# Rows without a number column, values ahead of the back transposes, and three routing steps a place, in a chunk-attention, top-1 MoE and SiLU-MLP kernel

## The chip, the cores and the metric

The kernel runs on one core of one Trainium2 chip, as one program. Its engines are TensorE (PE; PEld is its weight load), VectorE (DVE), ScalarE (ACT), GpSimd (POOL) and SyncE (SP, which issues most DMAs). They run side by side, each through its own list of instructions in order, and wait for one another on semaphores. The metric is the time of one execution in microseconds on the device; lower is better.

## The reference: what is computed

Three layers follow one another, in float32. Chunked attention with 8 memory keys, a window of 16 to the left and 8 to the right:

```python
B, H, S, D = 4, 8, 768, 64
for c in range(S // 32):
    q_c = q[:, :, c * 32:c * 32 + 32]
    k_full = concat([mem_k, k[:, :, max(0, c * 32 - 16):min(S, c * 32 + 40)]])
    v_full = concat([mem_v, v[:, :, ...]])
    a = softmax(q_c @ k_full^T / sqrt(D))
    out[:, :, c * 32:c * 32 + 32] = a @ v_full
x = out.transpose(0, 2, 1, 3).reshape(3072, 512)
```

Then a mixture of 8 experts, of which each token takes the best one, with a gate from normalised logits:

```python
logits = unit(x) @ unit(expert_emb).T / tau
expert_idx = argmax(logits, axis=1)
gate_w = softmax(logits)[arange(N), expert_idx]
for e in range(8):
    out[mask_e] = gate_w[mask_e] * (relu(x[mask_e] @ w1[e]) @ w2[e])   # 512 -> 1024 -> 512
```

Then a dense MLP, `h = x @ w_in` (512 to 2048), `h * sigmoid(h)`, `@ w_out` (2048 to 512).

## The kernel before, in words

The order of the work on every engine is written out by hand, by the order in which the Python code records instructions.

**Attention** (`scores`, `exps`, `turned`, `values`, `columns`, `logits`, `logits2`) runs in 32 units `u`. A unit is one pair of heads (4 pairs a batch, 4 batches) and one half of the sequence, 384 tokens. In the loop over `u` several units are in flight: `scores(u)` multiplies q with the windows of k (PE, L780), DVE takes the maximum and subtracts it (L789, L792), ACT takes the exponential (`exps`, L797), `turned(u-1)` transposes the last unit's weights (PE, L803) and copies them (ACT, L805), `values(u-2)` multiplies by v (PE, L815) and DVE divides into `xb` (L827 to L831), and `columns(u-3)` transposes the result (PE, L849) and copies it to `xs` (ACT, L850). DVE and ACT also lay out the windows of k for the next pair (`kbuf`, L708). After the last pair of heads of a half, `logits(u-3)` multiplies `xs` by the expert vectors (PE, L864), DVE copies that (`ls`, L873), and `logits2(u-4)`, in the next unit, transposes it back (PE, L881) for a sum on DVE (L883). So two units of each batch hold a `logits` and the two after them a `logits2`. The half's rows are written from `xb` to the DRAM buffer `xd` by SP (L839).

`xd` has 3072 rows of 513 numbers, 2052 bytes: 512 values and the token's number, which POOL copies into `xb` (L825). `ys`, the DRAM buffer of the experts' results, has rows of the same form.

**Routing** is a list of small generators (`ranks`, `leading`, `places`, `gates`, `compact`) in `pending`. `advance(n)` runs the next `n` steps (up to each `yield`) at a place in the other work. `RATE`, here 2, is the number of steps at a place from the fifth unit before the last on. A step that yields `HOLD` keeps the next one back until a later place where PE may be used. `leading` picks two experts' first 256 tokens each (`pre`, two slots of two tiles of 128 rows): it ends in `pre_i`, a list of token numbers (L346), from which POOL gathers rows of `xd` (`gather`, L148). `places` then puts every other token at a place in slots of three or two tiles and leaves `ixs`, the token number at each of NA = 34 x 128 places. `compact` makes `rows_i`, the places in use, by way of the tile `wideh` (L558 to L564).

**The experts** run slot by slot (`step`, `firsts`, `seconds`), eight slices of the hidden layer each. Weights arrive in float32 and are split in a high and a low part by ACT and DVE (L92, L93); each product is three matmuls (`three`, L97 to L99). `turn` transposes the gathered rows (L170) and splits them. `first_mm` copies the number column aside (`ids`, L176), `second_mm` copies it behind the results (L196), and `put` writes the tile to `ys` (L201).

**The MLP** takes tokens in groups of four tiles. `pick` gathers a tile from `ys` (L1048), `pick_gate` takes the number column as integers (`tok_i`, L1056) and gathers the gates from `gd` by it (L1057), `gated` scales, `turn2` transposes, and `give` scatters the result by `tok_i` to the output (L1182).

Of the kernel before, what the change touches and what calls it, by code (L numbers as in the profile page):

```python
# [39 lines left out]
NF2 = FF2 // P  # L40
XW = DM + 1

# [16 lines left out]
def tile_chunk_attention_top1_moe_silu_mlp(ctx, tc, qT, kT, vW, emb, tau, wm, wo, out, dbg=None):  # L59
# [7 lines left out]
    psum = ctx.enter_context(tc.tile_pool(name="psum", bufs=1, space=PSUM))  # L67
    xd = dram.tile([N, XW], F32, name="xd")
    NY = N3 * 3 * P + N2 * 2 * P
    ys = dram.tile([NY + 3 * P, XW], F32, name="ys")  # L70
    gd = dram.tile([N, 1], F32, name="gd")
    bank = [psum.tile([P, DM], F32, name=f"bank{i}") for i in range(8)]

# [14 lines left out]
    meta_i = const.tile([1, LAST2 + 1], I32, name="meta_i")  # L88
    ids = const.tile([P, 3, 1], F32, name="ids")

# [26 lines left out]
    def space(pool, tag, nt):  # L117
        xs = tuple(pool.tile([P, KD, nt * P], F32R, name=f"x{n}{tag}") for n in "hl")
        hs = [tuple(pool.tile([P, nt * P], F32R, name=f"h{n}{tag}{i}") for n in "hl") for i in range(2)]
        return dict(x=xs, h=hs, row=pool.tile([P, nt, XW], F32, name=f"xrow{tag}"))  # L120

# [51 lines left out]
    def first_mm(s, f):  # L173
        n = s.nt * P
        if f == 0:
            DVE.tensor_copy(ids[:, 0:s.nt], s.where["row"][:, 0:s.nt, DM:])  # L176
        wh, wl = w1s[f % 2]
        xh, xl = s.where["x"]
        h = bank[2 + f % 2][:, 0:n]
        for k in range(KD):  # L180
            c = slice(k * P, (k + 1) * P)
            three(h, (wh[:, c], wl[:, c]), (xh[:, k, 0:n], xl[:, k, 0:n]), k == 0, k == KD - 1)
        hh, hl = (t[:, 0:n] for t in s.where["h"][f % 2])
        ACT.activation(hh, h, AF.Relu)  # L184
        DVE.scalar_tensor_tensor(hl, h, 0.0, hh.bitcast(F32), op0=ALU.max, op1=ALU.subtract)  # L185

    def second_mm(s, f):
        hh, hl = s.where["h"][f % 2]
        for c in range(s.nt):
            t = slice(c * P, (c + 1) * P)  # L190
            three(bank[s.acc + c], (hh[:, t], hl[:, t]), w2_of(s, f), f == 0, f == NF - 1)
        if f == NF - 1:
            y = s.y()
            for c in range(s.nt):
                if c == 1:
                    DVE.tensor_copy(y[:, 0:s.nt, DM:], ids[:, 0:s.nt])  # L196
                (DVE.tensor_copy if c % 2 else ACT.copy)(y[:, c, 0:DM], bank[s.acc + c])

# [285 lines left out]
    def places(home):  # L484
# [55 lines left out]
        for k in range(1, N3 + 1):  # L540
            out_ = rows2_i if k == N3 else ixp
            DVE.scalar_tensor_tensor(out_, ixs[:, 3 * k:3 * k + NA], here[:, k:k + 1], ixp, op0=ALU.mult, op1=ALU.add)
            yield

    def compact():

# [119 lines left out]

    SPOTS, HOLD, RATE, LASTW, GP = (2, 6), 2, 2, 1, 2

# [6 lines left out]
    with ExitStack() as a:  # L675
# [132 lines left out]
        def values(u):  # L808
# [14 lines left out]
            if half == 0 and pr == 0:  # L823
                xb[b] = xp.tile([P, TPB, XW], F32, tag="xb", name=f"xb{b}")
                POOL.tensor_copy(xb[b][:, :, DM:], token[:, b * TPB:(b + 1) * TPB])  # L825
            den = sm.tile([P, G, 2, 1], F32, tag="den", name=f"den{u}")
# [64 lines left out]
        for u in range(NU + 2):  # L891
# [8 lines left out]
            if u == 4:  # L900
                expert_columns()
            if 0 <= u - 4 < NU - 2 and place(u - 4)[3] == NPAIR - 1:
                logits2(u - 4)
            if ahead < NJ:
# [5 lines left out]
            if 0 <= u - 1 < NU:  # L910
                turned(u - 1)
            if 0 <= u - 3 < NU:
                columns(u - 3)
            if 0 < u < NU:
                exps(u)
            if 0 <= u - 2 < NU and u != NU:
                values(u - 2)
            advance(1 if u < NU - 5 else RATE, pe=True)
            if 0 <= u - 3 < NU and place(u - 3)[3] == NPAIR - 1:
# [26 lines left out]
        for i in range(1, NF - 2):  # L946
            ahead_of(pre[0], i)
            firsts(pre[0], i)
            if i == 1:
                logits2(NU - 1)  # L950
                pending.extend([places(bank[6]), gates(), compact()])
            seconds(pre[0], i)
            for b, t in squares[:2]:
                square(b, t)
            del squares[:2]
    lg = ex.enter_context(tc.tile_pool(name="lg", bufs=1, side="right"))
    large = [space(lg, "l", 3)]
    large.append(dict(large[0], x=tuple(lg.tile([P, KD, 3 * P], F32R, name=f"x{n}m") for n in "hl")))
    yfirst = [lg.tile([P, 2, XW], F32, name=f"yfirst{n}") for n in range(2)]
    w2d = tuple(lg.tile([P, DM], F32R, name=f"v2{n}3") for n in "hl")  # L960
# [22 lines left out]
    ypool = ctx.enter_context(tc.tile_pool(name="ypool", bufs=1))  # L983
    ymore = ypool.tile([P, 4, XW], F32, name="ymore")
    POOL.memset(ymore, 0.0)
# [14 lines left out]
    yr = [y[:, c] for y in yfirst for c in range(2)]  # L1000
    tok_i = [yrow.tile([P, TG], I32, name=f"tok{g}") for g in range(NG)]
    gt = [yrow.tile([P, TG], F32, name=f"gt{i}") for i in range(2)]
# [43 lines left out]
    def pick(g, c):  # L1046
        t = (g - 1) * TG + c
        POOL.indirect_dma_start(  # L1048
            out=yr[c],
            out_offset=None,  # L1050
            in_=ys[0:NA * P],
            in_offset=IndirectOffsetOnAxis(ap=rows_i[:, t:t + 1], axis=0),
        )

    def pick_gate(g, c):
        DVE.tensor_copy(tok_i[g][:, c:c + 1], yr[c][:, DM:])  # L1056
        POOL.indirect_dma_start(  # L1057
# [239 lines left out]
```

## Time and profile before

| | us |
|---|---|
| median of 3 runs | 1032.03 (1029.16 to 1032.31) |
| profiled execution | 1033.47, its span 1031.8 |
| PE busy | 977.9 (95%) |
| DVE busy | 617.2 (60%) |
| ACT busy | 463.9 (45%) |
| POOL busy | 147.4 (14%) |
| granted TensorE clock, mean | 0.988 |

Busy times are of the profiled execution. A row of a timeline gives start, duration, engine, line, operation, output<-input, and in brackets for how long the engine stood idle before it and which work ended that wait. PEclk is the clock that TensorE was granted, as a share of full speed, and a DMA share is the mean busy share of the 16 DMA engines.

### The profile page before, as it was taken

To read this page: it belongs to the slowest core of one execution; us is meant where nothing else is said; L and a number is where in the kernel's file an instruction comes from. 1 tells how busy PE (TensorE), PEld (TensorE's weight loads), DVE (VectorE), ACT (ScalarE), POOL (GpSimd) and SP (SyncE) were. 2 spreads that over 40 slices of the span, in tenths; PEclk is the share of its full clock that TensorE was granted. 3 is DMA by queue.
4 is the path that set the end of the run, shared out by engine and by line. 5 is a ranking of instruction groups with operands and counts; after the bars stand their busy time and mean duration, and the time that the engine had idled before them with its cause. 6 is when DMAs were issued, how large, how long until landed. Compare 5 with 4: busy or idle time off the path is not lost. (4 is left out here: it accounts for less than half of the span.)

```text
span 1031.8 us, 16881 instructions
## 1 busy us (share of the span) xinstructions
PE 977.9 (95%) x6365; PEld 824.8 (80%) x6365; DVE 617.2 (60%) x1274; ACT 463.9 (45%) x890; POOL 147.4 (14%) x209
## 2 busy tenths in 40 slices
PE   6788798999999999998999999999999999999995
PEld 4566677899988989997878888888888888888884
DVE  8788788777777888895999952332332232223230
ACT  8667566454456565664453433222322332232230
POOL 6133122110002000100310002021021002101001
PEclk9999999999999999999999999999999999999998
DMA  8989756664678887877443301020011002001001
GB/s 303 285 262 287 255 164 223 206 215 159 199 240 253 261 261 244 276 228 227 149 123 102 102 1 41 1 82 1 1 49 34 1 11 72 1 1 42 1 1 41
DMA packets 43537, 139.40 MB, mean 135 GB/s; under 512 B 5780, under 2 KB 5804, under 8 KB 43444
## 3 DMA queue, kind: packets, MB, share of 16 engines
q1 hardware_dynamic: 36596, 118.24, 35.7%
q0 software_dynamic: 6848, 19.97, 6.4%
q8 instruction: 53, 0.87, 0.3%
q14 instruction: 40, 0.33, 0.1%
HBM read 115.33 MB, written 22.85 MB: 134 GB/s over the span
## 5 line engine op out<-in xcount | busy, mean ns | idle before, releaser
L1159 DVE TENSOR_TENSOR sg<-bank,sg 128x512 f32<-128x512 f32 x96 | 66.2, 690 | 222.0 <-ACT sg L1154 222.0
L1154 ACT ACTIVATE sg<-bank 128x512 f32<-128x512 f32 x96 | 57.3, 597 | 258.9 <-PE bank L99 258.9
L93 DVE TENSOR_TENSOR gl<-sg,gh 128x512 fp32r<-128x512 f32 x92 | 63.8, 693 | 51.7 <-ACT gh L92 50.2
L97 PE MATMUL bank<-yh,w2bh 128*128 128x512 f32 x240 | 94.5, 394 | 0.0
L99 PE MATMUL bank<-yh,w2bl 128*128 128x512 f32 x240 | 93.5, 390 | 0.0
L98 PE MATMUL bank<-yl,w2bh 128*128 128x512 f32 x240 | 93.4, 389 | 0.0
L92 ACT CAST gh<-sg 128x512 fp32r<-128x512 f32 x92 | 57.1, 621 | 67.1 <-DVE sg L1159 67.1
L97 PE MATMUL bank<-w2bh,gh 128*128 128x512 f32 x224 | 87.3, 390 | 0.0
L99 PE MATMUL bank<-w2bh,gl 128*128 128x512 f32 x224 | 87.2, 389 | 0.0
L98 PE MATMUL bank<-w2bl,gh 128*128 128x512 f32 x224 | 87.1, 389 | 0.0
L97 PE MATMUL bank<-v2h,hhl 128*128 128x512 f32 x200 | 81.0, 405 | 0.0
L93 DVE TENSOR_TENSOR w1l<-raw,w1h 128x512 fp32r<-128x512 f32 x106 | 73.0, 689 | 12.6 <-ACT w1h L92 9.5
L184 ACT ACTIVATE hhl<-bank 128x256 fp32r<-128x256 f32 (+1 forms) x88 | 36.3, 412 | 95.6 <-PE bank L99 91.6
L99 PE MATMUL bank<-v2h,hll 128*128 128x512 f32 x200 | 79.0, 395 | 0.0
L98 PE MATMUL bank<-v2l,hhl 128*128 128x512 f32 x200 | 78.8, 394 | 0.0
L93 DVE TENSOR_TENSOR v2l<-raw,v2h 128x512 fp32r<-128x512 f32 x106 | 72.9, 688 | 0.0
L97 PE MATMUL bank<-xhl,w1h 128*128 128x256 f32 (+1 forms) x224 | 68.5, 306 | 1.4 <-DVEq L1124 1.4
L98 PE MATMUL bank<-xll,w1h 128*128 128x256 f32 (+1 forms) x224 | 68.4, 306 | 1.4 <-DVE xll L93 1.4
L185 DVE SCALAR_TENSOR_TENSOR hll<-bank,hhl 128x256 fp32r<-128x256 f32 (+1 forms) x88 | 40.3, 458 | 49.0 <-ACT hhl L184 48.5
L99 PE MATMUL bank<-xhl,w1l 128*128 128x256 f32 (+1 forms) x224 | 68.3, 305 | 0.0
L92 ACT CAST v2h<-raw 128x512 fp32r<-128x512 f32 x106 | 65.8, 621 | 1.2 <-PE bank L99 1.2
L92 ACT CAST w1h<-raw 128x512 fp32r<-128x512 f32 x106 | 65.1, 614 | 2.3 <-DMA raw<-in_wm_dram 2.3
(309 smaller groups left out, 2334.1 us busy)
## 6 DMA issues: line engine op xcount, KB each, us to landing
raw<-in_wm_dram SPq DMA_DIRECT2D x109, 512.0 KB, 4.6
coded<-in_wo_dram SPq DMA_DIRECT2D x36, 512.0 KB, 4.4
vbuf<-in_vW_dram SPq DMA_DIRECT2D x32, 390.0 KB, 6.2
k<-in_kT_dram SPq DMA_DIRECT2D x16, 400.0 KB, 7.5
xd<-xb SPq DMA_DIRECT2D x8, 769.5 KB, 7.7
q<-in_qT_dram SPq DMA_DIRECT2D x16, 384.0 KB, 6.0
ys<-ymore SPq DMA_DIRECT2D x8, 513.0 KB, 8.0
ys<-yfirst SPq DMA_DIRECT2D x7, 513.0 KB
```

The source lines that it names most:

```text
L92: ACT.copy(hi, src)
L93: eng.tensor_tensor(lo, src, hi.bitcast(F32), op=ALU.subtract)
L97: PE.matmul(out, lhsT=lh, rhs=rh, start=start, stop=False)
L98: PE.matmul(out, lhsT=lh, rhs=rl, start=False, stop=False)
L99: PE.matmul(out, lhsT=ll, rhs=rh, start=False, stop=stop)
L184: ACT.activation(hh, h, AF.Relu)
L185: DVE.scalar_tensor_tensor(hl, h, 0.0, hh.bitcast(F32), op0=ALU.max, op1=ALU.subtract)
L1154: ACT.activation(sg, h, AF.Sigmoid)
L1159: DVE.tensor_tensor(sg, h, sg, op=ALU.mult)
```

## The change: three things

1. The number column goes: rows of `xd`, `ys` and the tiles have 512 numbers (2048 bytes), and the copies into and out of the column go with it. Instead `names`, a new generator between `gates` and `compact`, transposes `ixs` and writes it to a DRAM buffer `td`, with `wideh` as its staging tile; `pick` gathers the numbers from `td` with a second indirect DMA. The first group's numbers are `pre_i` itself.
2. In the loop over units, `columns(u-3)` moves from before `exps(u)` and `values(u-2)` to behind them, and `logits2(u-4)` from before the windows of k to behind `turned(u-1)`.
3. `RATE` is 3 instead of 2.

```diff
-    xd = dram.tile([N, XW], F32, name="xd")
+    xd = dram.tile([N, DM], F32, name="xd")
...
-    ys = dram.tile([NY + 3 * P, XW], F32, name="ys")
+    ys = dram.tile([NY + 3 * P, DM], F32, name="ys")
...
+    td = dram.tile([NA * P, 1], I32, name="td")
...
     def first_mm(s, f):
         n = s.nt * P
-        if f == 0:
-            DVE.tensor_copy(ids[:, 0:s.nt], s.where["row"][:, 0:s.nt, DM:])
...
             for c in range(s.nt):
-                if c == 1:
-                    DVE.tensor_copy(y[:, 0:s.nt, DM:], ids[:, 0:s.nt])
-                (DVE.tensor_copy if c % 2 else ACT.copy)(y[:, c, 0:DM], bank[s.acc + c])
+                (DVE.tensor_copy if c % 2 else ACT.copy)(y[:, c], bank[s.acc + c])
...
+    def names():
+
+        yield HOLD
+        by_tile = bank[7][0:NA, 0:P]
+        PE.transpose(by_tile, ixs[:, 0:NA], ident)
+        yield
+        names_t = wideh.rearrange("p t e -> p (t e)")[0:NA, 0:P].bitcast(I32)
+        DVE.tensor_copy(names_t, by_tile)
+        SP.dma_start(out=td.rearrange("(t p) o -> t (p o)", p=P), in_=names_t)
+        yield
...
-    SPOTS, HOLD, RATE, LASTW, GP = (2, 6), 2, 2, 1, 2
+    SPOTS, HOLD, RATE, LASTW, GP = (2, 6), 2, 3, 1, 2
...
-                xb[b] = xp.tile([P, TPB, XW], F32, tag="xb", name=f"xb{b}")
-                POOL.tensor_copy(xb[b][:, :, DM:], token[:, b * TPB:(b + 1) * TPB])
+                xb[b] = xp.tile([P, TPB, DM], F32, tag="xb", name=f"xb{b}")
...
-            if 0 <= u - 4 < NU - 2 and place(u - 4)[3] == NPAIR - 1:
-                logits2(u - 4)
             if ahead < NJ:
                 windows(ahead, 1, u % 2)
                 windows(ahead, 0, u % 2)
...
                 turned(u - 1)
-            if 0 <= u - 3 < NU:
-                columns(u - 3)
+            if 0 <= u - 4 < NU - 2 and place(u - 4)[3] == NPAIR - 1:
+                logits2(u - 4)
             if 0 < u < NU:
                 exps(u)
             if 0 <= u - 2 < NU and u != NU:
                 values(u - 2)
+            if 0 <= u - 3 < NU:
+                columns(u - 3)
             advance(1 if u < NU - 5 else RATE, pe=True)
...
-                pending.extend([places(bank[6]), gates(), compact()])
+                pending.extend([places(bank[6]), gates(), names(), compact()])
...
-    tok_i = [yrow.tile([P, TG], I32, name=f"tok{g}") for g in range(NG)]
+    tok_i = [yrow.tile([P, TG], I32, name=f"tok{g}") if g else pre_i for g in range(NG)]
...
+        POOL.indirect_dma_start(
+            out=tok_i[g][:, c:c + 1],
+            out_offset=None,
+            in_=td,
+            in_offset=IndirectOffsetOnAxis(ap=rows_i[:, t:t + 1], axis=0),
+        )
 
     def pick_gate(g, c):
-        DVE.tensor_copy(tok_i[g][:, c:c + 1], yr[c][:, DM:])
```

How the order moves at three places. First PE at the logits of the first batch, before (bank_75 is the logits' bank, e the scores' exponentials, xb the attention's result, et the transposed weights):

```order
L864 MATMUL bank_75<-xs_0_391,enT 32x384 x4
L780 MATMUL bank_68<-kbuf_204,q_521 32x128 x12
L881 MATMUL bank_75<-ident,ls_0_719 128x128 x3
L803 MATMUL bank_71<-ident,e_682 128x128 x3
L849 MATMUL bank_74<-ident,xb_360 128x128 x3
L815 MATMUL bank_72<-vbuf_206,et_691 32x130 x12
L864 MATMUL bank_75<-xs_1_449,enT 32x384 x4
```

and of the change, where bank_76 is that bank:

```order
L869 MATMUL bank_76<-xs_0_407,enT 32x384 x4
L786 MATMUL bank_69<-kbuf_204,q_520 32x128 x12
L809 MATMUL bank_72<-ident,e_681 128x128 x3
L886 MATMUL bank_76<-ident,ls_0_718 128x128 x3
L821 MATMUL bank_73<-vbuf_206,et_690 32x130 x12
L854 MATMUL bank_75<-ident,xb_360 128x128 x3
L869 MATMUL bank_76<-xs_1_465,enT 32x384 x4
```

The back transposes of the logits (ls) stand behind the score transposes (e), and the transposes of the result (xb), whose copy the logits read, stand between the values and the logits.

Second DVE in the last units of attention, where `leading` ends, before (ev to ah are steps of routing, den and xb the division, mx the next maximum):

```order
L334 TENSOR_SCALAR bh<-count,ab 128x128 x2
L827 TENSOR_SCALAR den_1856<-bank_73 128x6
L354 SCALAR_TENSOR_TENSOR ev<-count_of,down 128x8
L356 TENSOR_REDUCE e_141<-ev 128x1
L829 RECIPROCAL den_1856<-den_1856 128x6
L358 TENSOR_SCALAR two<-r_mv,e_141 128x18
L359 TENSOR_SCALAR chosen_i<-e_141 1x1
L361 SCALAR_TENSOR_TENSOR st<-two,ab 128x18
L831 TENSOR_TENSOR xb_1675<-bank_73,den_1856 128x3x128
L365 TENSOR_SCALAR ah_153<-st,row 128x18
...
L344 TENSOR_SCALAR ix_154<-bank_75 128x2
L789 TENSOR_REDUCE mx_1946<-bank_69 128x6
L346 TENSOR_TENSOR pre_i<-ix_154,bank_75 128x2
```

and of the change:

```order
L329 TENSOR_SCALAR bh<-count,ab 128x128 x2
L349 SCALAR_TENSOR_TENSOR ev<-count_of,down 128x8
L714 COPY kbuf_204<-k_1619 64x12x56
L351 TENSOR_REDUCE e_141<-ev 128x1
L353 TENSOR_SCALAR two<-r_mv,e_141 128x18
L354 TENSOR_SCALAR chosen_i<-e_141 1x1
L356 SCALAR_TENSOR_TENSOR st<-two,ab 128x18
L832 TENSOR_SCALAR den_1853<-bank_74 128x6
L360 TENSOR_SCALAR ah_153<-st,row 128x18
...
L339 TENSOR_SCALAR ix_154<-bank_76 128x2
L341 TENSOR_TENSOR pre_i<-ix_154,bank_76 128x2
L795 TENSOR_REDUCE mx_1958<-bank_70 128x6
```

The routing steps stand ahead of the division of that unit, and pre_i ahead of the last maximum.

Third DVE between the gates and the places in use, before (seg is the staging tile of the gates):

```order
L586 RECIPROCAL gate<-gate 128x24
L592 COPY seg<-bank_75 24x128
L547 TENSOR_TENSOR lens<-rem,wide 128x8
L549 TENSOR_TENSOR lens<-rem,lens 128x8
L405 SCALAR_TENSOR_TENSOR cends<-lens,countf 128x16
L407 TENSOR_TENSOR cfirst<-cends,lens 128x16
L553 TENSOR_TENSOR skip<-row_167,cfirst 128x8
L554 TENSOR_TENSOR skip<-row_168,cfirst 128x8
L558 TENSOR_TENSOR wideh<-token,cfirst 128x320
```

and of the change:

```order
L592 RECIPROCAL gate<-gate 128x24
L598 COPY seg<-bank_76 24x128
L547 CAST wideh<-bank_76 34x128
L553 TENSOR_TENSOR lens<-rem,wide 128x8
L555 TENSOR_TENSOR lens<-rem,lens 128x8
L400 SCALAR_TENSOR_TENSOR cends<-lens,countf 128x16
L402 TENSOR_TENSOR cfirst<-cends,lens 128x16
L559 TENSOR_TENSOR skip<-row_167,cfirst 128x8
L560 TENSOR_TENSOR skip<-row_168,cfirst 128x8
L564 TENSOR_TENSOR wideh<-token,cfirst 128x320
```

The copy of the numbers into wideh is new, and seven instructions later wideh is written again.

## Rows read from the trace of the kernel before

**Rows 1.** The page's busy times, shares of the span and instructions.

```profile
PE 977.9 (95%) x6365; PEld 824.8 (80%) x6365; DVE 617.2 (60%) x1274; ACT 463.9 (45%) x890; POOL 147.4 (14%) x209
```

**Rows 2.** Stretches: start:end and length, busy by engine (instructions), PEclk, DMA share, GB/s.

```profile
26.00:32.00 6.00, 5.60 (x140) 4.39 (x136) 5.50 (x14) 4.83 (x10) 1.16 (x4) 1.00 0.86 294
40.00:50.00 10.00, 5.10 (x111) 4.06 (x111) 5.71 (x19) 3.73 (x10) 1.31 (x4) 0.91 1.03 281
50.00:60.00 10.00, 9.86 (x168) 7.78 (x168) 7.75 (x22) 8.38 (x20) 1.76 (x6) 0.75 0.75 283
70.00:80.00 10.00, 7.36 (x142) 5.79 (x145) 7.84 (x23) 5.93 (x16) 1.31 (x4) 0.94 1.00 300
80.00:90.00 10.00, 9.59 (x199) 7.54 (x192) 8.36 (x25) 8.18 (x19) 2.36 (x7) 0.88 0.89 316
118.00:130.00 12.00, 8.92 (x54) 7.04 (x45) 6.62 (x15) 5.05 (x11) 0.00 (x0) 0.86 0.88 251
190.00:1031.80 841.80, 822.87 (x4129) 701.29 (x4127) 459.95 (x822) 338.88 (x626) 90.19 (x91) 0.99 0.34 109
```

**Rows 3.** Timeline of 33 to 49 us: the write to xd and a late k.

```profile
33.21 3.05 SPq L839 DMA_DIRECT2D xd<-xb  x2
...
48.17 0.51 DVE L708 COPY kbuf<-k 64x672 f32<-64x672 f32 x1 [3.25 <-DMA k<-in_kT_dram]
```

**Rows 4.** DMA: slices of 38:46, 486:494, 1021:1027 us; issues, KB each, us to landing.

```profile
DMA  9959999999979979397696999999159959799989
GB/s 123 133 123 226 154 174 164 123 113 103 82 103 133 108 92 103 51 135 99 58 161 151 183 178 193 117 225 115 63 195 348 353 174 316 251 292 442 364 348 427
...
GB/s 41 41 0 0 0 226 380 431 349 369 390 236 226 205 143 123 307 369 307 348 205 61 123 164 410 471 369 348 410 348 348 123 82 0 0 0 0 0 0 82
...
GB/s 0 0 0 0 0 0 0 0 0 0 0 0 0 0 55 355 410 410 410 109 0 0 0 0 0 0 0 0 0 0 0 0 0 0 0 0 0 0 0 0
...
raw<-in_wm_dram SPq DMA_DIRECT2D x109, 512.0 KB, 4.6
...
xd<-xb SPq DMA_DIRECT2D x8, 769.5 KB, 7.7
...
out_dram<-o,tok POOLq DMA_INDIRECT x24, 2.7
ymore<-ys,rows_i POOLq DMA_INDIRECT x20, 3.7
```

**Rows 5.** Timeline of 95 to 99 us: a unit that ends in logits.

```profile
95.72 0.89 PE L864 MATMUL bank<-xs,enT 128*32 128x384 f32 x8
...
97.39 0.55 DVE L789 TENSOR_REDUCE mx<-bank 128x6 f32<-128x384 f32 x1
97.52 0.31 PEld L881 LDWEIGHTS bank<-ident,ls 128*128 128x128 f32 x3 [0.53 <-DVE ls L873]
...
98.24 0.49 PE L849 MATMUL bank<-ident,xb 128*128 128x128 f32 x3
...
98.81 0.49 ACT L850 COPY xs<-bank 128x384 f32<-128x384 f32 x1
```

**Rows 6.** Timeline of 113 to 123 us: the first slot's gather.

```profile
113.41 0.14 DVE L346 TENSOR_TENSOR pre_i<-ix,bank 128x2 int32<-128x2 f32 x1
...
115.34 0.95 POOL L148 DMA_INDIRECT xrows<-xd,pre_i  x1 [0.30 <-issue]
...
122.92 1.48 PE L170 MATMUL bank<-ident,xrows 128*128 128x128 f32 x7 [2.49 <-DMA xrows<-xd,pre_i]
```

**Rows 7.** Timeline of 178 to 186 us: gates, places in use, first slot of three tiles.

```profile
178.84 0.66 PE L170 MATMUL bank<-ident,xrowl 128*128 128x128 f32 x4 [0.95 <-DMA xrowl<-xd,rows_i]
...
181.32 0.28 DVE L592 COPY seg<-bank 24x128 f32<-24x128 f32 x1 [0.37 <-PE bank L589]
...
181.63 0.36 SPq L593 DMA_DIRECT2D gd<-seg  x1
...
182.51 0.48 DVE L558 TENSOR_TENSOR wideh<-token,cfirst 128x320 f32<-128x320 f32 x1
...
185.98 0.44 PE L98 MATMUL bank<-xll,w1h 128*128 128x384 f32 x1 [1.43 <-DVE xll L93]
```

More of the change, by code (lines that the diff above doesn't have):

```diff
@@ L40 @@
 NF2 = FF2 // P
-XW = DM + 1
 TS = 2
@@ L88, in tile_chunk_attention_top1_moe_silu_mlp @@
     meta_i = const.tile([1, LAST2 + 1], I32, name="meta_i")
-    ids = const.tile([P, 3, 1], F32, name="ids")
     def split(src, hi, lo, eng=DVE):
@@ L119, in space @@
         hs = [tuple(pool.tile([P, nt * P], F32R, name=f"h{n}{tag}{i}") for n in "hl") for i in range(2)]
-        return dict(x=xs, h=hs, row=pool.tile([P, nt, XW], F32, name=f"xrow{tag}"))
+        return dict(x=xs, h=hs, row=pool.tile([P, nt, DM], F32, name=f"xrow{tag}"))
     NCO = 2
@@ L958, in tile_chunk_attention_top1_moe_silu_mlp @@
     large.append(dict(large[0], x=tuple(lg.tile([P, KD, 3 * P], F32R, name=f"x{n}m") for n in "hl")))
-    yfirst = [lg.tile([P, 2, XW], F32, name=f"yfirst{n}") for n in range(2)]
+    yfirst = [lg.tile([P, 2, DM], F32, name=f"yfirst{n}") for n in range(2)]
     w2d = tuple(lg.tile([P, DM], F32R, name=f"v2{n}3") for n in "hl")
@@ L983, in tile_chunk_attention_top1_moe_silu_mlp @@
     ypool = ctx.enter_context(tc.tile_pool(name="ypool", bufs=1))
-    ymore = ypool.tile([P, 4, XW], F32, name="ymore")
+    ymore = ypool.tile([P, 4, DM], F32, name="ymore")
     POOL.memset(ymore, 0.0)
```

## The prediction

> **What bounds the kernel now.** I read the page's busy times first: TensorE (PE) is busy for 977.9 of 1031.8 us [rows 1], so only the time in which it stands idle, or runs at half its clock, can be won. The table of stretches [rows 2] says where that is. From 190 us on PE is busy for 822.87 of 841.80 us; what is left there is mostly the joins of the branches and what follows the last matmul, and the change touches neither. So its place is before 190 us. In the attention units (10 to 118 us) VectorE (DVE) sets the pace: in a clean piece (26 to 32 us) it is busy for 5.50 of 6.00 us, a share of 0.917. The reader is to see that other stretches fall short of that share: 5.71, 7.75, 7.84 and 8.36 us in four windows of 10 us, with the DMA engines at shares of 1.03, 0.75, 1.00 and 0.89 and PE's granted clock at 0.75 to 0.94.
>
> The views of waits and of DMA say why. SP issues the two writes of one batch's attention rows to xd at 33.21 us [rows 3]; at 48.17 DVE has stood 3.25 us for a load of k that queued behind them [rows 3]. From 38 to 46 us the DMA engines are busy nearly all the time and move some 100 to 150 GB/s, and at the end of that window, with loads alone, over 350 [rows 4]. One such write of 769.5 KB lands after 7.7 us, a load of 512 KB after 4.6, and a scatter of 256 KB in rows of 2048 bytes to the output after 2.7, its bytes moving at 410 GB/s [rows 4]. The rows of xd have 2052 bytes. So I read the slow stretch as a slow write of rows with an odd length, which holds up the loads behind it.
>
> **The change, part by part.** The sum is made against the profiled execution: 1033.47 us, span 1031.8. That execution lies 1.44 us above the median of the three runs, 1032.03, to which I carry the difference over.
>
> *A, rows of 2048 bytes in xd.* Bytes fall by 0.2%, which is nothing; what counts is the rate of the write. By the clean share of 0.917, the four stretches lack 9.17 - 5.71 = 3.46, 1.42, 1.33 and 0.81 us of DVE work, in all 7.02 us, and 7.02 / 0.917 = 7.7 us of time [rows 2]. If a pair of writes goes at the rate of the output's scatter, 1.57 MB at 410 GB/s take 3.8 us, where the rate is low now from the issue until about 44 us, and k is no longer late. If the rate stays, nothing is won. The ends are 0 and -7.7. The scatter is the nearest row for a write with this row length, though it is only 256 KB at a time. I take three quarters, **-5.8**.
>
> The Trainium skill (DMA: Bandwidth & Descriptors, How a descriptor splits into AXI transactions) speaks against that: a row that starts off a 256-byte boundary costs only the bytes back to that boundary, at worst 2304 instead of 2048 bytes moved, 12% more; by that rule A would be near nothing and the sum near the first rival's. The trace disagrees so far, in that the rate there differs by a factor of three to four at the same DMA share [rows 4], but it has no long write in rows of 2048 bytes.
>
> *B, values ahead of the transposed results.* In a plain unit this moves PE work that DVE hides: DVE has hardly an idle moment in a clean piece, so it costs and gives nothing there. It matters in the two units per batch that end in the router's logits. There PE now runs values, logits (95.72), next scores, and DVE's next maximum follows at 97.39, right behind PE [rows 5]. In the new order the transposes of the results (0.49 us, 98.24) stand between values and logits, and the logits need their copy by ACT (0.49 us, 98.81) [rows 5], which in the old order ran beside the values. That adds 0.49 + 0.49 and about 0.1 of hand-offs, less the 0.49 for which the values no longer wait: 0.6 us, twice a batch. The back transposes of the logits, moved behind the score transposes, no longer make PE wait for DVE (0.53 us at 97.52) [rows 5], which I take off once a batch. That is 1.2 - 0.53 = 0.67 a batch; three batches lie in the DVE-paced part: **+2.0**, with ends 0 (all hidden) and 3 x 1.2 = +3.6.
>
> *C, three steps a place.* This moves DVE work of the router forward by some rows in the last five units; its amount stays. The PE place of the row-choosing matmuls is held by the code, so the list of rows (pre_i, 113.41) comes only one DVE instruction earlier, about 0.5 us. What counts is the gather behind it: issued by POOL at 115.34, it frees PE at 122.92, 7.6 us later, and PE stands 2.49 us [rows 6]; the like gather from ys lands in 3.7 [rows 4]. Between those two issues lies an xd write again. With A's faster write the gather would be there at 115.34 + 3.7 = 119.0, before PE comes to it at 122.92 - 2.49 = 120.4, and PE starts by that wait earlier: **-2.5**. Ends: 0 (the write stays slow), and -4, if the clock, 0.86 in 118 to 130 us [rows 2], is not lowered in the shorter gap either.
>
> *D, the list of token numbers (td).* One PE transpose, one DVE copy and one DMA are added, just after the gates' own at 181.32 [rows 7]. The transpose uses the same bank and waits for the gates' copy (0.28), then DVE copies (0.28): 0.6 us on both engines. The staging tile is wideh, which DVE rewrites soon after (182.51) [rows 7]: that instruction now waits until the DMA to td has read it and landed. Queued behind it on DVE are the weight splits and the split of xrowl for the first slot of three tiles, and PE already waits 1.43 us for that split at 185.98 [rows 7]. Issued at about 182.2 and landing after 2.7 us, as the scatter does [rows 4], the DMA ends at 184.9, against 183.1 for a rewrite that is late by the 0.6 alone: 1.8 + 0.6 = 2.4. SP is free then, since it issues the gates' DMA at 181.63, right behind their copy [rows 7], and so small a DMA may land quicker; I take **+2.0**. Ends: +0.6 (it lands at once) and +6 (it lands as late as an xd write, 7.7).
>
> *E, the gather for the slot of three tiles.* PE stands 0.95 us for it at 178.84 [rows 7]; with writes to ys and reads of xd in whole rows it should land earlier: **-0.9**, ends 0 and -0.95.
>
> *F, the rest, at nothing.* The copies of the number (xb on POOL; ids, the y column and tok on DVE) go, on engines with room: after 190 us DVE is busy for 459.95 of 841.80 us [rows 2]. Twenty gathers of numbers come on POOL's queue, 20 x (0.95 + 0.30) = 25 us at the price of a gather's issue [rows 6], with POOL busy for 90 of those 841.80 us [rows 2]. Behind them in the queue stand gate gathers and output scatters; the gate gathers gain in turn, since they no longer wait for a DVE copy between matmul steps. If that cover were gone, a group's gates would come 4 x 1.25 = 5 us later.
>
> Sum: -5.8 + 2.0 - 2.5 + 2.0 - 0.9 = **-5.2**: 1028.3 for the profiled execution, **1026.8** for the median.
>
> **The rivals.** First, *the write to DRAM is slow whatever the row length*: it collapses because 1.57 MB come at once. For this speaks that a single write of 513 KB in rows of 2052 bytes (486 to 494 us) moves at 350 to 430 GB/s [rows 4]; against it the 7.7 us that a write of 769.5 KB takes. Then A and E are 0 and C is the 0.5 alone, and the additions decide: +2.0 + 2.0 - 0.5 = +3.5, **1035.5**, slower. It decides from the point at which A's relief falls under about 3.5 us.
>
> Second, *the write gets faster, but the loads do not gain as much*: in a clean piece the DMA share is already 0.86 [rows 2], so a batch's 1.57 MB still push some loads past their unit. A halves to -2.9 and C to -1.3: -2.9 + 2.0 - 1.3 + 2.0 - 0.9 = -1.1, **1031**, no change.
>
> Third, *everything late was late by those writes*: A -7.7, C -4, E -0.9, and B and D at +1 each, as DVE then has slack in the logits units: -10.6, **1021.4**.
>
> **How the numbers follow.** Chances: forecast 0.45, first rival 0.20, second 0.20, third 0.15. The predicted time is the forecast's, 1026.8; its own range, with A from -3.5 to -7.7, C to -4 and D from +0.6 to +4, is 1022 to 1031. The range of eight in ten reaches over the third rival with B at 0 and D at +0.6, 1020.0, and up to the first: 1019.5 to 1035.5; what it leaves out is half of the first rival and a little beyond the third. A measurement of this kernel can tell about 0.3%, 3.1 us. Faster by more than that: nine tenths of the forecast, all of the third, a quarter of the second, 0.60. Within it: a tenth of the forecast, most of the second, two fifths of the first, 0.27. Slower: mostly three fifths of the first, 0.13.
>
> **What would show it.** Right, for A: xd writes landing in under 5 us, DVE near 0.9 in all windows from 40 to 90 us, no wait of DVE for k over 1 us. For B: PE waiting for ACT's copy before each logits, and these units longer by 0.6 us. For C: PE's wait for xrows near 0. For D: DVE waiting for a DMA at the rewrite of wideh, and PE's wait for the split growing by 2. Wrong, if the DMA rate behind an xd write is still near 100 GB/s, or if PE idles in new places after 190 us, at the gates of the output groups.

## The result: 0.7% slower, where a gain of 0.5% was forecast

| | before | after |
|---|---|---|
| median of 8 runs each | 1030.67 (1029.16 to 1033.07) | **1036.71** (1035.44 to 1043.76) |
| ratio, 95% interval | | 1.0069 [1.0052, 1.0086] |
| profiled execution, its span | 1033.47, 1031.8 | 1036.38, 1034.4 |

The kernel before differs from chip to chip (medians 1026.3 to 1030.7), so each experiment below is given as a ratio to runs of it on the same chip. The profiled execution of before, at 1033.47, took longer than any of its eight runs, so part of a lead that another trace has over it can be that execution's own.

The page of after, busy times, against [rows 1]: PE is busy 13 us longer for one instruction more, POOL 21 us longer, DVE and ACT no longer than before.

```profile
PE 990.8 (96%) x6366; PEld 820.6 (79%) x6366; DVE 616.1 (60%) x1225; ACT 460.7 (45%) x890; POOL 168.0 (16%) x225
```

The same stretches of after as in [rows 2] (start:end and length, busy by engine, clock, DMA share, GB/s):

```profile
40.00:50.00 10.00, 9.95 (x199) 6.95 (x197) 8.71 (x26) 7.72 (x18) 2.44 (x8) 1.00 1.00 371
50.00:60.00 10.00, 9.11 (x193) 6.35 (x188) 9.18 (x28) 8.07 (x20) 1.76 (x4) 1.00 0.85 293
70.00:80.00 10.00, 9.58 (x212) 6.94 (x214) 9.25 (x29) 8.72 (x22) 1.73 (x7) 1.00 0.97 359
80.00:90.00 10.00, 8.99 (x165) 5.82 (x153) 9.00 (x25) 6.98 (x16) 5.31 (x11) 1.00 0.73 258
118.00:130.00 12.00, 11.42 (x82) 9.56 (x83) 8.96 (x32) 7.17 (x18) 0.00 (x0) 1.00 0.62 198
190.00:1034.40 844.40, 828.02 (x4099) 697.29 (x4097) 453.21 (x770) 335.31 (x622) 111.06 (x110) 1.00 0.32 106
```

Up to 130 us the signs of the forecast are there: DVE's four windows hold 8.71, 9.18, 9.25 and 9.00 us for 5.71, 7.75, 7.84 and 8.36, and the clock is at its upper level throughout. The DMA view of 38 to 46 us and the landing of an xd write, against [rows 4]:

```profile
GB/s 164 399 369 399 389 369 348 287 205 215 225 205 236 195 187 368 432 432 384 539 422 437 437 468 312 468 406 468 374 308 369 430 430 416 381 464 384 416 478 552
DMA packets 1031, 2.95 MB, mean 369 GB/s; under 512 B 99, under 2 KB 99, under 8 KB 1030
...
xd<-xb SPq DMA_DIRECT2D x8, 768.0 KB, 4.5
```

Where the time then went is read by putting the same PE instruction of both traces side by side; the difference of their starts, after minus before:

| at (us of before) | 125 | 150 | 190 to 475 | 573 | 617 | 695 | 703 | 785 | 789 | 875 | 879 | 970 | 1018 | end of the span |
|---|---|---|---|---|---|---|---|---|---|---|---|---|---|---|
| difference (us) | -7.0 | -7.8 | -6 | -4.1 | -4.1 | -2.5 | -0.3 | +1.2 | +3.3 | +4.3 | +6.3 | +8.0 | +8.4 | +2.6 |

So after is 7.8 us ahead of this trace at 150 us and gives back 1.7 at the routing up to 190. Then **14.2 us are lost between 480 and 1020 us, in the MLP, where the forecast put nothing**. The loss has two forms: steps, of 1.3 us at about 503 and of 2.1 to 2.2 at 700, 787 and 877, 7.7 in all; and a creep between them (1.6 us from 617 to 695, 1.5 from 703 to 785), the other 6.5. At the very end 5.8 us come back.

The waits of PE in 480 to 1020 us (what waited <- for what: us in total, times, longest), of before and of after, show the steps as a wait that before does not have, for ACT's upper half `gh` of an activation:

```profile
PE bank L97 <- DVEq L1124: 4.1, 1, 4.1
PE bank L97 <- DVE held L1174: 1.7, 1, 1.7
```

```profile
PE bank L96 <- ACT gh L91: 4.4, 4, 1.5
PE bank L96 <- DVE held L1184: 1.6, 1, 1.6
```

At the first step, POOL (678 to 694 us) and ACT (684 to 700 us) of after:

```profile
688.04 0.94 POOL L1059 DMA_INDIRECT tok<-td,rows_i  x1 [0.30 <-issue]
689.29 0.94 POOL L1067 DMA_INDIRECT gt<-gd,tok  x1 [0.30 <-issue]
690.53 0.95 POOL L1067 DMA_INDIRECT gt<-gd,tok  x1 [0.30 <-issue]
691.79 0.94 POOL L1067 DMA_INDIRECT gt<-gd,tok  x1 [0.30 <-issue]
693.03 0.94 POOL L1067 DMA_INDIRECT gt<-gd,tok  x1 [0.30 <-issue]
```

```profile
687.41 0.62 ACT L91 CAST gh<-sg 128x512 fp32r<-128x512 f32 x1 [0.76 <-issue]
696.53 0.60 ACT L1164 ACTIVATE sg<-bank 128x512 f32<-128x512 f32 x1 [8.51 <-remote]
```

Twelve gathers (four rows, four numbers, four gates) go out back to back from 679.21. ACT's sigmoid at 696.53 waits 8.51 us; the matmul it waits for ends at 691.55, but its semaphore is seen to rise only at 696.45. In before the gates of that group are 5.44 us apart, each released by DVE's copy of a token number:

```profile
702.66 0.94 POOL L1057 DMA_INDIRECT gt<-gd,tok  x1 [15.46 <-DVE tok L1056]
708.10 0.94 POOL L1057 DMA_INDIRECT gt<-gd,tok  x1 [4.50 <-DVE tok L1056]
```

### The profile page after: what moved, and what is told of

Same layout as the page of the kernel before. It is cut to its first block, busy times and chain, and to the rows that moved or that the text cites. A ratio compares the mean times of both kernels' runs of the same rounds, so it can differ in the third digit from the quotient of the medians.

```text
span 1034.4 us, 16856 instructions
## 1 busy us (share of the span) xinstructions
PE 990.8 (96%) x6366; PEld 820.6 (79%) x6366; DVE 616.1 (60%) x1225; ACT 460.7 (45%) x890; POOL 168.0 (16%) x225
## 5 line engine op out<-in xcount | busy, mean ns | idle before, releaser
L96 PE MATMUL bank<-yh,w2bh 128*128 128x512 f32 x240 | 95.1, 396 | 0.0
L96 PE MATMUL bank<-w2bh,gh 128*128 128x512 f32 x224 | 87.4, 390 | 0.0
L1192 POOL DMA_INDIRECT out_dram<-o,tok x20 | 20.6, 1030 | 389.8 <-DVE o L1189 348.6
L96 PE MATMUL bank<-v2h,hhl 128*128 128x512 f32 x200 | 80.4, 402 | 0.0
L147 POOL DMA_INDIRECT xrowl<-xd,rows_i x28 | 31.0, 1108 | 243.2 <-PE bank L169 201.2
L96 PE MATMUL bank<-xhl,w1h 128*128 128x256 f32 (+1 forms) x224 | 68.7, 307 | 1.4 <-DVEq L1134 1.4
```

Of the source, the lines that this page charges most:

```text
L96: PE.matmul(out, lhsT=lh, rhs=rh, start=start, stop=False)
L147: POOL.indirect_dma_start(out=s.where["row"][:, c], out_offset=None, in_=xd[0:LEAD * P] if s in pre else xd, in_offset=IndirectOffsetOnAxi ...
L1192: POOL.indirect_dma_start(out=out, out_offset=IndirectOffsetOnAxis(ap=tok_i[g][:, c:c + 1], axis=0), in_=o, in_offset=None,)
```

## The experiments

The theories. **Addresses**: the column's removal moved SBUF tiles, and the matmuls run slower with operands at other addresses (the creep). Worked out from the tiles' sizes, `w2a`, one half of the MLP's weights, moved from byte 27616 to 27552 of its partition (modulo 256: from 224 to 160), and `yh`, the activations, from 77024 to 76928 (224 to 128); the other operands are at 224 in both kernels. **Bursts**: gathers issued back to back hold up the semaphores of other engines (the steps). Rivals: the bursts alone make both; or the new order of instructions or DVE's changed load does.

**e1, after with two unused tiles**, which put `w2a` and `yh` back at 224 modulo 256 and change no instruction:

```diff
     ymore = ypool.tile([P, 4, DM], F32, name="ymore")
+    ypool.tile([P, 16], F32, name="pad1")
...
     yrow = ctx.enter_context(tc.tile_pool(name="yrow", bufs=1))
+    yrow.tile([P, 8], F32, name="pad2")
```

> The changed kernel with two unused tiles of 64 and 32 bytes, which put the second layer's first weights (w2a) and the transposed rows of the even groups (yh, yl) back at the distance from the other operands that they had before (equal to them modulo 256 bytes). Theory 1, the matmuls of the MLP got slower (233 instead of 227 ns from start to start) because the two SBUF operands of a matmul no longer agree in their address: the 233 goes back to 227 and the time falls by 6 to 9 us, to about 1029. Rival, the 233 comes from the added gathers on POOL's queue or from their traffic: the cadence and the time stay as in the changed kernel, 1036.7. Rival 2, addresses matter, but for one of the two tiles alone: 2 to 5 us.

**e2, after with the number copied by DVE ahead of each gate gather**, as before, so that gates are paced again:

```diff
+    tok_t = yrow.tile([P, NG, TG], I32, name="tok_t")
...
-            out=tok_i[g][:, c:c + 1],
+            out=tok_t[:, g, c:c + 1],
...
+        if g:
+            DVE.tensor_copy(tok_i[g][:, c:c + 1], tok_t[:, g, c:c + 1])
```

> The changed kernel with one small copy by VectorE between the gather of a token's numbers and the gather of its gates, as the old kernel had it, so that POOL can no longer issue a group's twelve gathers back to back; no address of a matmul's operand moves. Theory 2, the three stalls of 2 us at 700, 790 and 880 us and the one of 1 us at 503 us come with those bursts: they go, and the time falls by 5 to 7 us, to about 1030. Rival, they come from something else at a group's change (the scatters, the fetch of code): they stay, and the time stays at 1036.7 or rises a little by the copies.

**e3, both edits.**

> Both edits together. If theories 1 and 2 hold and are independent, the time falls by 13 to 15 us against the changed kernel, to about 1022, which is 8 us under the kernel before: the part up to 190 us was 6 us ahead of it. If one of them is wrong, it falls by the other alone. If the gain up to 190 us is an accident of one profile, the time ends near 1030.

**e4, before with two unused tiles**, which bring `w2a` and `yh` to after's remainders, 160 and 128:

```diff
     ymore = ypool.tile([P, 4, XW], F32, name="ymore")
+    ypool.tile([P, 48], F32, name="pad1")
...
+    yrow.tile([P, 56], F32, name="pad2")
```

> The kernel before with two unused tiles of 192 and 224 bytes, which put w2a and yh at the changed kernel's distances modulo 256 bytes and leave every instruction as it is. Theory 1: its matmuls of the MLP go from 227 to some 233 ns in the same stretches as in the changed kernel, and the time rises by 6 to 9 us, to about 1038. Rival, the cadence comes from the gathers: no change, 1030.7.

Measured, on one chip: e1 **0.9914** [0.9895, 0.9934], e2 1.0000 [0.9985, 1.0014], e3 0.9942 [0.9921, 0.9963], e4 **1.0056** [1.0039, 1.0074]. e4 is before with nothing but addresses changed, and costs 5.8 us. Its windows against those of before (columns as in [rows 2]; before first, then e4):

```profile
614.00:695.00 81.00, 81.00 (x367) 67.23 (x366) 25.82 (x42) 23.46 (x39) 15.66 (x16) 1.00 0.12 40
695.00:798.00 103.00, 103.00 (x463) 85.28 (x463) 30.46 (x50) 28.46 (x47) 13.40 (x14) 1.00 0.07 21
840.00:979.00 139.00, 139.00 (x625) 115.07 (x624) 41.01 (x64) 38.29 (x64) 15.45 (x16) 1.00 0.07 23
```

```profile
614.00:695.00 81.00, 81.00 (x360) 65.96 (x359) 26.34 (x42) 22.77 (x38) 15.32 (x15) 1.00 0.12 39
695.00:798.00 103.00, 103.00 (x456) 83.92 (x455) 29.27 (x48) 27.86 (x46) 13.43 (x14) 1.00 0.07 21
840.00:979.00 139.00, 139.00 (x613) 113.03 (x612) 40.02 (x62) 36.92 (x62) 15.48 (x16) 1.00 0.07 23
```

PE is busy all the time in both, at full clock, yet gets through 7, 7 and 12 matmuls fewer in e4. That is 26 of some 227 ns, 5.9 us. So the addresses are shown to be the creep. In e1 it is gone: its PE starts lie 8.8 us ahead of before's at 573 us and 8.7 at 1017. In e2 it stays, from -4.8 to +1.6 us over the same stretch.

But e1 also lost the steps, with its bursts untouched, so this chip does not decide on the bursts; e3 paces what here cost nothing, and pays 1.45 us at 513 to 533 us for the later gates of the first gathered group. The next runs were on another chip, with after itself as a control.

**e5, after again; e6 and e7, after's rows with before's order** of the attention loop, addresses aligned as in e1, and two (e6) or three (e7) routing steps a place:

```diff
-    SPOTS, HOLD, RATE, LASTW, GP = (2, 6), 2, 3, 1, 2
+    SPOTS, HOLD, RATE, LASTW, GP = (2, 6), 2, 2, 1, 2
...
+            if 0 <= u - 4 < NU - 2 and place(u - 4)[3] == NPAIR - 1:
+                logits2(u - 4)
...
+            if 0 <= u - 3 < NU:
+                columns(u - 3)
             if 0 < u < NU:
```

> The changed kernel once more, on the chip and in the session of the next three. In its first profile it stood for 2 us at 700, 790 and 880 us; the kernel with the two pads (e1_aligned) has the same bursts of twelve gathers and no such stall. Theory 3, the stalls belong to that session and not to the change: here the changed kernel has none, and its time is that of e2_paced against the kernel before, ratio 1.000. Rival, they come with the addresses, too: they are there again, and the ratio is 1.007 as first measured.

> The kernel with the pads (e1_aligned), with the order of the attention units as before and two routing steps a place, so that of the change the rows of 512 and the list td are left. The forecast's terms A, D and E, -5.8 + 2.0 - 0.9 = -4.7, would give a ratio to the kernel before of 0.9955; full relief (A -7.7, D as measured +0.8, E -0.9) 0.992; if the rows give nothing and the new order all, 1.000 or more.

> The kernel with the pads, with the order of the attention units as before; three routing steps a place stay. The forecast's term B says that the new order costs 2.0 us: then this is 2 us faster than e1_aligned, ratio 0.989. If the new order is worth something (values no longer wait behind the transposes), it is slower than e1_aligned by 1 to 3 us, ratio 0.993 to 0.995. If it is hidden, 0.991.

Measured: e5 1.0068 [1.0045, 1.009], e6 1.0036 [1.0018, 1.0055], e7 1.0054 [1.0034, 1.0073]. All three have steps at the bursts: in e5 of 1.7, 2.1 and 1.9 us (none at 787), in e6 and e7 of 2.6 to 4. So the new order does not make them. In the step of 4 us, e6's at 700, the granted clock is also at its lower level (1.2 GHz) for 3.4 us.

**e8, the matmul by itself**: PE alone runs 128x512 matmuls on 100 pairs of addresses, 24 on each pair, one line of code for each difference modulo 256:

```diff
+                if (w - m) % 256 == 0:
+                    PE.matmul(bank[n % 4], lhsT=wbase[:, w // 4:w // 4 + P], rhs=base[:, m // 4:m // 4 + DM], start=k == 0, stop=k == REP - 1)
+                elif (w - m) % 256 == 32:
...
```

> Nothing but matmuls of 512 columns, 24 for each of 100 pairs of start addresses: the moving operand at 0, 32, ... 224, 256 and 512 bytes past one address and the stationary one likewise; one source line for each difference modulo 256 bytes. The output isn't computed. If theory 1 holds with the difference modulo 256 as its rule, the line of difference 0 runs at 227 ns from start to start and the others at 230 to 238; if modulo 128, the lines of 0 and 128 run alike; if only the address of one operand counts, the eight lines run alike in the mean and the cases of one moving address differ; if nothing of it holds, all run at 227.

Four neighbours on e8's timeline, one line for each pair or two (L94 is difference 192, L96 is 224, L82 is 0, L84 is 32; the last line is cut off by the end of the view):

```profile
116.63 5.65 PE L94 MATMUL bank<-moving,still 128*128 128x512 f32 x24
122.12 5.76 PE L96 MATMUL bank<-moving,still 128*128 128x512 f32 x24
127.71 5.61 PE L82 MATMUL bank<-moving,still 128*128 128x512 f32 x24
133.16 2.02 PE L84 MATMUL bank<-moving,still 128*128 128x512 f32 x8
```

From start to start, 24 matmuls take 5.49, 5.59 and 5.45 us: 228.8, 232.9 and 227.1 ns each. Over all pairs the median is 227 ns at difference 0, 229 at 192, and 232 to 234 at the other six. PE was the only engine at work, so this is no contention with another. The Trainium skill (SBUF — State Buffer, SBUF: two separate sides) says that PE never waits on another engine for SBUF. These runs don't speak against that; but 1 to 3% of a matmul's rate hang on where its own two operands lie.

**e9 and e10, after and e1 once more on a third chip; e11, e7 with e2's pacing; e12, the gathers of numbers and gates all moved forward** into the experts, from 283 us on, with a tile of its own to stage td:

```diff
+    def pick_name(g, c):
...
-            for do, at in (pick, 1), (pick_gate, 3), (gated, 4), (turn2, 5 + c // 2):
+            for do, at in (pick, 1), (gated, 4), (turn2, 5 + c // 2):
...
+            tail[twos[0 if n < 10 else 1], 2 + n % 10 // 2].append(lambda g=g, c=c: pick_name(g, c))
+            tail[twos[2 if n < 10 else 3], 2 + n % 10 // 2].append(lambda g=g, c=c: pick_gate(g, c))
```

> The changed kernel, as control beside the next. e1_aligned had bursts of twelve gathers and no stall, on another chip than e5_control, which had the stalls. If the stalls belong to the chip or the session, this one and e10_aligned_again have them both or neither of them: ratios 1.007 and 0.999, or 1.000 and 0.991. If they belong to the kernel, this one has them and e10 has not: 1.007 and 0.991.

> The kernel of e1_aligned once more, in one session with the control; see there. The matmuls of the MLP run at 227 ns either way.

> The kernel of e7_no_reorder (pads, the old order of the attention units, three steps a place) with the small copy that paces the gathers of the gates. e7 was at 1.0054 with three stalls of 2.7 us and one of 1.3 in its profile. If those are the bursts' and the new order is worth nothing, this is at 0.994 like e3_both, which differs from it by the new order alone; if the new order costs the forecast's 2 us, at 0.992; if it is worth 14 us, as e7 against e1_aligned would have it, still above 1.000.

> The changed kernel with the gathers of the token numbers and of all gates moved ahead into the expert slots, where POOL is idle, so that a group of the MLP gathers its four tiles and nothing else; with the addresses put right, and a staging tile of its own for the list of numbers. If the bursts make the stalls and the first group's late gates cost e3_both its 1.5 us at 520 us, both are gone: ratio 0.989 to 0.992 in any session. If not, 0.994 like e3_both.

Measured: e9 1.0117 [1.0102, 1.0132], e10 1.0083 [1.007, 1.0096], e11 **0.9975** [0.9961, 0.999], e12 **1.0294** [1.027, 1.0318]. e10 is the kernel of e1, and comes out 1.7% apart from it. PE's waits in 480 to 1020 us of e1, then of e10:

```profile
PE bank L96 <- DVE held L1186: 0.5, 1, 0.5
```

```profile
PE bank L96 <- ACT gh L91: 6.6, 3, 2.3
PE bank L96 <- issue: 1.5, 2, 1.0
PE bank L98 <- issue: 0.9, 1, 0.9
PE bank L96 <- ACT held L1186: 0.4, 1, 0.4
```

The same PE instructions of these two lie 1.4 us apart at 458 us, and 5.7, 8.6, 11.3 and 14.1 us apart behind the four bursts: 4.3, 2.8, 2.8 and 2.8 us for one burst each, and between bursts not a tenth. In the first of these steps e10's granted clock is also at its lower level for 3.4 us. So the steps belong to the bursts, but not in every session: on the chip of e1 to e4 the same burst cost nothing. e12 speaks for it from the other side. Its MLP has no steps, but PE loses 36 us at its four bursts, of 16, 12, 12 and 12 gathers, between 283 and 400 us, 10 of them at one matmul. Part of the 36 is the clock's, which is at its lower level for 30.6 us of that stretch. The waits of PE in 283 to 345 us:

```profile
PE bank L96 <- issue: 11.3, 2, 9.6
```

e11 on the same chip has its gates paced and no steps. Pacing takes only the four gates out of a burst of 12; the eight gathers of rows and numbers still go out back to back, and there cost nothing.

**e13, before with rows of 512 in `xd` alone.** The number that `ys` needs in its rows is copied from the list of indices that the gather of those rows uses, so `ys` keeps its column, there is no `td`, and no gather is added; unused tiles hold the expert and MLP operands at 224:

```diff
-    xd = dram.tile([N, XW], F32, name="xd")
+    xd = dram.tile([N, DM], F32, name="xd")
...
-        if f == 0:
-            DVE.tensor_copy(ids[:, 0:s.nt], s.where["row"][:, 0:s.nt, DM:])
...
-                if c == 1:
-                    DVE.tensor_copy(y[:, 0:s.nt, DM:], ids[:, 0:s.nt])
+                DVE.tensor_copy(y[:, c, DM:], s.rows(c))
```

> The kernel before with one part of the change, rows of 512 in xd (and in the tiles that are written to it and gathered from it): the number that goes into the rows of ys is copied from the list by which the row was gathered, so that neither td nor its twenty gathers are needed; unit order and two steps a place as before; unused tiles keep all operands of the experts and the MLP equal modulo 256 bytes. If the gain up to 190 us is the rows' alone, and the losses behind it come from addresses and bursts alone, it keeps the whole gain: ratio 0.989 to 0.992 in any session. If the new order or the third step had a part in the gain, 0.993 to 0.996; if the losses have another cause, 1.000.

**e14 is e3 again, e15 is e11 again, and e16 is e3 with two steps a place**, for what the new order and the third step are worth:

> The kernel of e3_both (changed kernel, addresses put right, gates paced), which had 0.994, as the base for the next two in one session; 0.994 to 0.997.

> e14 with the old order of the attention units. Term B of the forecast, +2.0 us for the new order: this is 0.002 below e14. Rival, the new order costs nothing: equal to e14 within 0.001. Rival, it gains: 0.002 above.

> e14 with two routing steps a place in place of three. Term C of the forecast gave the third step 0.5 us at most (the list of rows one instruction earlier) and the rest of its 2.5 to the faster write: equal to e14 within 0.001. If the third step is worth something, 0.002 or more above; if it crowds the units, below.

Measured, on one chip: e13 **0.9932** [0.9907, 0.9957], e14 0.9934 [0.9909, 0.996], e15 0.9922 [0.9896, 0.9947], e16 0.9933 [0.9907, 0.9959]. All four beat the kernel before by the same 0.7 to 0.8%. In the total, the new order (e14 against e15) and the third step (e14 against e16) cannot be told from nothing, and rows of 512 in `xd` with the addresses held bring a gain of this size by themselves. The equal times hide unequal parts. At the end of PE's work e13 is 8.9 us ahead of before's trace, and e14, e15 and e16 only 5.1, 5.3 and 8.0; but these three have the shorter end of the span that comes next. And e15 is the kernel of e11, which measured 0.9975 on its chip: the intervals do not overlap, and why is open.

**e17 and e18, e13 with some gate gathers done twice**, for the 5.8 us at the end of the span. The last scatter to the output is issued 10.1 us before the end of the span in before, and 4.2 in after:

```profile
core 0 of [0], span 1031.8 us
...
1021.70 0.97 POOL L1182 DMA_INDIRECT out_dram<-o,tok  x1 [3.00 <-ACT o L1179]
```

```profile
core 0 of [0], span 1034.4 us
...
1030.17 0.97 POOL L1192 DMA_INDIRECT out_dram<-o,tok  x1 [3.12 <-ACT o L1189]
```

The trace's last long instruction is POOL's closing drain: 9.46 us in before, e4 and e13, which issue 100 indirect DMAs, and 3.56 to 3.58 in after and every other kernel above that issues 120. e17 issues 120, e18 110:

```diff
-        POOL.indirect_dma_start(
+        for _ in range(2 if g and c < 4 else 1):
+            POOL.indirect_dma_start(
```

> e13_from_list with every gate of the groups 1 to 5 gathered twice, 20 gathers more that nobody waits for, 120 indirect DMAs in all as in the changed kernel instead of 100. POOL's closing drain lasted 9.46 us in the three kernels with 100 of them and 3.57 us in the four with 120 that were looked at. If the number of indirect DMAs sets it, the drain here is 3.57 us and the time some 5.9 us under e13's: ratio 0.987. If it is the gathers of td or another part of the change, the drain stays at 9.46 and the ratio at 0.993; it rises if the gathers get in the way of the scatters.

> The same with the gates of two of a group's four tiles gathered twice, 110 indirect DMAs. If the drain falls evenly with their number, it is 6.5 us here and the ratio 0.990; if it is a matter of a count that is passed or not, 9.46 or 3.57, or something else again.

Measured: e17 1.0052 [1.004, 1.0064], e18 1.0017 [1.0007, 1.0027]. The drain took 3.58 us in e17 and 10.28 in e18, so its length goes with the number of indirect DMAs, and not in proportion. The extra gathers do not pay: they delay the gates of the first gathered group, and PE starts 12.2 us (e17) and 7.3 (e18) later at 497 to 522 us, with the granted clock at its lower level for 10.2 and 6.8 us there.

## Why the prediction was wrong, step by step

**A, -5.8: right in its mechanism, open in its size.** All three signs are there: the write lands in 4.5 us, DVE is at 0.87 to 0.93 in the four windows, and no wait for k above the 1 us named is left there. The first rival, in which the write stays slow whatever the row length, is excluded: in 38 to 46 us the DMA engines move 369 GB/s on average, against 182 in before. That is also more than the 12%, an estimate that the prediction worked out for rows off a 256-byte boundary from the Trainium skill (DMA: Bandwidth & Descriptors, How a descriptor splits into AXI transactions); the page says it of reads, and these are writes.

The size was read from one execution of before. e4 is a second one with the same attention and rows of 2052 bytes. Its write is slow too (238 GB/s in the same window), yet DVE does more in the four windows:

```profile
40.00:50.00 10.00, 7.29 (x146) 5.65 (x150) 8.07 (x24) 6.35 (x16) 1.31 (x4) 0.94 1.00 325
50.00:60.00 10.00, 9.50 (x192) 7.31 (x184) 8.26 (x24) 7.92 (x17) 2.65 (x8) 0.89 0.87 306
70.00:80.00 10.00, 8.54 (x175) 6.29 (x178) 9.21 (x26) 8.32 (x21) 2.41 (x8) 1.00 1.03 407
80.00:90.00 10.00, 8.48 (x185) 6.45 (x189) 9.27 (x27) 7.04 (x16) 6.46 (x15) 1.00 0.91 315
...
xd<-xb SPq DMA_DIRECT2D x8, 769.5 KB, 8.3
```

By the prediction's own reckoning e4 lacks 1.10 + 0.91 = 2.0 us of DVE work, not 7.02, and A would be -2.2. PE in e4 is 6.4 us ahead of before's trace at 102 us, with no change to the rows. So of the 8.9 us by which e13 leads that trace at 100 us, most can be that execution's own: over e4 the lead is 2.6 at 102 us and 1.1 at 190. What holds is the total of e13, 0.9932 [0.9907, 0.9957], that is 7.0 us [4.4, 9.6].

**B, +2.0: the wait came, the time did not stay.** PE waits for ACT's copy before the logits, as predicted: 0.71 us at 115.41. With the new order (e14) PE is 6.3 us ahead of before's trace at 102 us, without it (e13, e15) 9.0: 2.7 for three batches. But at 126 us e14 and e15 are 0.7 apart, and e14 against e15 is 0.0012 of the whole, inside the intervals. Most of B is given back when attention runs out. A likely reason, not tested alone: in six of the seven traces with the old order and rows of 2048 bytes the granted clock falls to its lower level for 3.4 us or more at 101 to 104 us, and in nine of the ten with the new order it does not fall there.

**C, -2.5: right.** The two gathers go out at 109.03 and 110.52 instead of 113.86 and 115.34 (the second is in [rows 6]), and PE starts on them at 116.17 without a wait (in e4, with rows of 2052 bytes, it waits 1.58 us there):

```profile
116.17 1.09 PE L169 MATMUL bank<-ident,xrows 128*128 128x128 f32 x8
```

That comes from A's faster write; the third step by itself adds nothing (e16).

**D, +2.0: the sum came out, the parts did not.** The rewrite of wideh waits 0.55 us and not 1.8, since the DMA to td lands at once; PE's wait for the split grows by 0.6 us against [rows 7], not by 2:

```profile
176.37 0.49 DVE L564 TENSOR_TENSOR wideh<-token,cfirst 128x320 f32<-128x320 f32 x1 [0.55 <-DMA td<-wideh]
...
179.84 0.44 PE L97 MATMUL bank<-xll,w1h 128*128 128x384 f32 x1 [2.06 <-DVE xll L92]
```

From 175 to 190 us, four of the 13 traces with td staged in wideh, after among them, give back 1.1 us (E's gain included), and the other nine 2.6 to 2.7; the three without td (e13, e17, e18) give back nothing. In the nine the granted clock falls to its lower level for 3.4 us behind PE's wait, which the forecast did not have. So in e14:

```profile
178.00:182.00 4.00, 3.60 (x12) 3.60 (x13) 2.52 (x5) 1.51 (x3) 3.24 (x4) 0.57 0.73 247
```

**E, -0.9: the wait for that gather is gone**, but PE now waits 1.1 us for the gates and 0.4 for `seg` at the same place, where before did not, so that a net gain is not shown.

**F, "the rest, at nothing", is the step that failed**, twice. First, "the copies of the number (xb on POOL; ids, the y column and tok on DVE) go, on engines with room" prices a column by its instructions. It also has a place in SBUF, and each tile allocated behind it moves; that cost about 6.5 us here in the MLP (5.8 in e4, which moves the two tiles alone). No trace row of before could have shown the price; the sizes in the diff could have shown that the tiles move. Second, of the 20 gathers it says that POOL has room, and "the gate gathers gain in turn, since they no longer wait for a DVE copy". POOL did have room. But that wait was what kept the gathers apart. Without it they went out in bursts of 12, which cost mostly 2 to 3 us each where they cost anything: 7.7 us in all in after. The page's totals, 90 us of POOL's 841.80, say nothing of the density. The prediction's own sign of being wrong, that "PE idles in new places after 190 us, at the gates of the output groups", came near: PE idles at the bursts that hold those gates, but for `gh`.

Against the sum of -5.2, after was 6.1 us ahead at 190 us, but of that one trace of before. F, put at 0, was +14.2, and the end of the span, which no term had, -5.8. The medians lie 6.0 apart; an estimate from that, 6.0 - 14.2 + 5.8, leaves about -2.4 for A to E, under half of what was forecast. The first rival's 1035.5 lies close to the measured time, for a reason that was false.

Left open: why a burst costs mostly 2 to 3 us in the sessions of after, e5 to e7, e9 and e10, and nothing in that of e1. In such stretches the trace also lacks some of PE's semaphore updates, so that how much of ACT's 8.51 us is a late semaphore and how much a late record can't be said; PE's own lost time is measured either way.

## What to carry to other kernels

When a change removes or adds a few bytes per row, work out where every later tile lands, and hold the matmul's two operands at the same address modulo 256 with an unused tile; test it by moving addresses alone. Before pricing a removed wait at a gain, ask what it kept apart on the queue behind it. A control of the unchanged kernel belongs in each session: one kernel here was 0.9914 on one chip and 1.0083 on another.

## What was not expected of the hardware

- A matmul with 512 columns starts every 227 ns if its moving and stationary operands agree modulo 256 bytes, every 229 at difference 192, and every 232 to 234 otherwise (e8); in a whole kernel that was 0.56% (e4).
- Gathers issued back to back by POOL stall engines that have nothing to do with them: bursts of 12 for 1.3 to 2.2 us each in after and about 2.8 more in e10 than in e1, bursts of 12 to 16 in the experts for 36 us in all, a lowered clock included (e12), and none in the session of e1.
- POOL's closing drain took 9.46, 10.28 and 3.57 us with 100, 110 and 120 indirect DMAs in the program.
